# A spectral block's forward and backward pass: full tiles for one-row operands, half-column pairs as fill, and new hand-written orders

## The chip, the cores and the metric

The kernel runs on one core of a Trainium2 chip. A core has a matrix engine (TensorE, "PE" in the rows of the profile, with its weight loads as "PEld"), a vector engine (VectorE, "DVE"), a scalar engine (ScalarE, "ACT"), a general engine (GpSimd, "POOL") and a queue engine that only starts transfers (SyncE, "SP"). The metric is the time on the device in microseconds (us). The median of three runs of the kernel before the change is 398.4 us (397.93 to 398.51). The profiled execution is a single one and has its own time.

## The reference

The kernel computes one block's output and all its gradients, in bf16, with S = 2048 rows, D = 512 columns and F = 1792 hidden columns:

```python
mod = (silu(c) @ w_mod)               # six rows of 512: sa, ca, ga, sb, cb, gb
h   = layernorm(x) * (1 + ca) + sa
x   = x + ga * irfft2(rfft2(h) * (w_r + 1j * w_i))
h   = layernorm(x) * (1 + cb) + sb
out = x + gb * (relu(h @ w1 + b1) ** 2 @ w2 + b2)
```

It returns `out` and, for a given gradient of `out`, the gradients of x, w_r, w_i, w1, b1, w2, b2, c and w_mod. The gradient of w_mod is the outer product of silu(c) with six column sums over all 2048 rows; the gradient of c needs the same sums.

## The kernel before, in words

The 2048 rows are 16 row tiles of 128 (NT), in four row blocks of 512 (NB); the 1792 hidden columns are 14 chunks of 128 (NFC). Both Fourier transforms are matmuls with tables of sines and cosines that the kernel makes itself. PE's work, in time:

- **Start, to about 17 us.** Loads of c, w_mod, x, the output's gradient (`gT`, transposed by the load, four blocks) and w2 (`w2T`, transposed too, four parts). Ten matmuls of constants run first (L731 to L733). `vrow`, the row c, is transposed to a column; silu of it multiplies the blocks of w_mod (`mod_row`, L754, and for block 5 L769, which gives `gb2x`, the factor of the output's gradient). Block 5 is loaded from ACT's queue, the rest from SP's.
- **First spectral product, to about 51 us.** For each pair of row tiles: statistics and scaling of the layernorm, a fold on DVE (L267, L268), the product with the table TA (psA, L303 and L304). As fill, `back_products` (L858): for each row block b and chunk fc, four matmuls 128x128 by 128x512 give w2 transposed times the scaled gradient. `scale_g` (L777) scales `gT` first. At the end of the stage one-row products make `dcrow` (psd, L837) and the columns `mcol` (L842).
- **spec_f23, forward, 51 to 75 us.** Eight groups; each has 16 matmuls psB (L345, 128 rows by 64 columns of the array, in pairs side by side at column 0 and 64), an evaluation AE on ACT (L349), a small patch of AE on POOL (L351), then two times four matmuls psC (L328, also 128 by 64), cast on ACT (Xs, L329) and multiplied with the filter on DVE. Two matmuls of one row (`dcrow` by `ind`, L340) add the shift in the first group. Back products are the fill.
- **spec_g1, 75 to 84 us.** The inverse transform's first part, psG (L375), 64 rows by 128 columns.
- **MLP forward and backward, 84 to 263 us.** Products of 128 by 128 by 512 (L1029, L1059 and others), with column sums (`colsums`, L924) of 32 columns each, four side by side, into one PSUM tile `acc`. After it, rows 0, 32, 64 and 96 of `acc` are the sums for four blocks of w_mod; they are copied to `grow` and `gcrow`.
- **Backward spec_f23 and spec_g1, 263 to 324 us.** The same matmuls as forward; the fill is `grad_w1` (L1303): 16 units of 16 matmuls, eight of 512 columns and eight of 384. `grad_b1` (L1254) goes with one of them. `GMod.emit` (L478) spreads one row of `grow` over 128 partitions with a one-row matmul, then multiplies (ACT, DVE) and writes the gradient of w_mod.
- **Row gradient and grad_w2, 324 us to the end.** Products for the gradient of x, with column sums (L1460), `grad_w2` (L1402) as fill, and the last two `GMod.emit`, from `acc1_sb`.

What runs when is written out by hand. `ORDER` has a list for each engine: the program issues its instructions in some order, and the list names them by their number in it; `set_order` ties each to the one before it on its engine. SP's list is thus the order in which transfers are started. No planner takes part when the kernel is built.

A tile on the array is given by the operand's rows and the weights' columns, and by `tile_position`; rows such as `128*64` in the profile name it.

Of the kernel before, what the change touches and what calls it, by code (L numbers as in the profile page):

```python
# [18 lines left out]
D = 512  # L19
# [3 lines left out]
NFC = 14  # L23
# [50 lines left out]
def build_basic(tc, constp):  # L74
# [14 lines left out]
    K["one0"] = one0  # L89
    pid = constp.tile([P, 1], I32, name="pid")  # L90
# [168 lines left out]


# [199 lines left out]
class GMod:  # L460
# [12 lines left out]
    def emit(self, jc, q, row, pool, ppool, nbuf=2, last=False):  # L473
# [4 lines left out]
        nc.tensor.matmul(psb, lhsT=K["ones_sq"][q:q + 1, :], rhs=row, start=True, stop=True, tile_position=(q, 0))  # L478
# [49 lines left out]
    ),  # L528
    "ACT": (
# [79 lines left out]
def kernel(  # L609
# [703 lines left out]
    for fp in range(0, NFB, 2):  # L1313
        for dc in range(4):
            for fb in (fp, fp + 1):
                units.append(lambda fb=fb, dc=dc: grad_w1(fb, dc))
# [261 lines left out]
```

## Time and profile before

| | |
|---|---|
| median of the runs | 398.4 us |
| profiled execution, its own time | 397.56 us |
| its span in the trace | 395.8 us |
| mean granted clock of TensorE | 0.983 |
| PE, DVE, ACT, POOL busy | 96%, 86%, 69%, 6% |
| instructions in the lists: PE, ACT, DVE, POOL, SP | 2749, 458, 774, 84, 310 |

The shares are means over stages with different limits, so the stages are to be read one by one. A matmul's busy time in a row runs from its start to its modelled end, so that consecutive matmuls overlap in it: the distance from one row's start to the next is what a matmul costs. "x4" in a timeline row means that four instructions in succession are put into one row.

### The profile page before, as it was taken

What the parts mean: (1) busy time and instruction counts of PE and PEld (TensorE: products, weight loads), DVE (VectorE), ACT (ScalarE), POOL (GpSimd) and SP (SyncE); (2) the same over time, 40 slices, a digit from 0 to 9 for tenths busy, and PEclk for the clock granted to TensorE, in tenths of its full rate; (3) what the DMA queues carried; (4) which work ended last, traced back from release to release, by engine and by line L of the source; (5) the groups of instructions that cost most, each with busy time, mean ns of one, the idle gap of its engine ahead of it and who ended that gap; (6) DMA issues with size and microseconds to landing.
All of it is one profiled execution on the core that took longest, in us unless ns stands there. A gap on an engine that the chain in (4) does not pass through costs nothing.

```text
span 395.8 us, 7650 instructions
## 1 busy us (share of the span) xinstructions
PE 379.5 (96%) x2723; PEld 189.0 (48%) x2749; DVE 339.8 (86%) x830; ACT 274.6 (69%) x489; POOL 22.5 (6%) x88
## 2 busy tenths in 40 slices
PE   4799999899999999999999999999999999999996
PEld 1255554455544444444444445446455565444454
DVE  4999978959998689988899899984898998999572
ACT  4469899979973189338824977538837569998482
POOL 7411001000000000000000000000002000000000
PEclk8599999999999999999999999999999999999999
DMA  8997999979389999979966777969999898999998
GB/s 277 215 195 202 276 207 211 335 174 284 99 228 217 226 229 255 187 171 215 246 149 108 217 183 195 300 188 252 333 249 304 238 310 196 180 242 233 285 294 293
DMA packets 141965, 91.00 MB, mean 230 GB/s; under 512 B 96098, under 2 KB 127848, under 8 KB 141416
## 3 DMA queue, kind: packets, MB, share of 16 engines
q1 hardware_dynamic: 141220, 89.93, 91.6%
q10 hardware_dynamic: 708, 0.59, 0.5%
q8 instruction: 21, 0.34, 0.3%
q14 instruction: 16, 0.13, 0.1%
HBM read 36.35 MB, written 33.19 MB: 176 GB/s over the span
## 4 chain that ended last, share of the span: by engine, by line
PE 70%; ACT 10%; DMA 6%; DVE 6%; issue 5%; POOL 1%; ACTq 0%; SPq 0%; POOLq 0%
PE og_0s L1059 11%; PE og_1s L1059 11%; PE mm_0s L1303 5%; PE mm_1s L1402 5%; PE mm_0s L1402 5%; PE mm_0s L858 4%; PE mm_1s L858 4%; PE mm_1s L1029 3%; DMA h_dram<-h2r 3%; PE mm_0s L1029 2%; PE mm_1s L1303 2%; DMA wm_2s<-in_w_mod_dram 2%; PE pst L1029 2%; DMA hn_0s<-h_dram 2%; PE psB L345 2%
## 5 line engine op out<-in xcount | busy, mean ns | idle before, releaser
L1029 PEld LDWEIGHTS <-w 128*128 128x128 bf16 x224 | 21.5, 98 | 26.9 <-issue 2.6
L1303 PEld LDWEIGHTS <-h_sb 128*128 128x128 bf16 x256 | 23.6, 98 | 21.7 <-issue 1.9
L1059 PEld LDWEIGHTS <-gab 128*128 128x128 bf16 x224 | 21.7, 98 | 25.1 <-DVE gab L1036 0.2
L858 PEld LDWEIGHTS <-w2T 128*128 128x128 bf16 x224 | 20.8, 98 | 23.8 <-issue 5.6
L1303 PE MATMUL mm_0s<-gab,h_sb 128*128 128x384 bf16 (+1 forms) x160 | 31.1, 343 | 0.0
L1059 PE MATMUL og_0s<-w1T,gab 128*128 128x512 bf16 x111 | 26.4, 379 | 0.1
L1059 PE MATMUL og_1s<-w1T,gab 128*128 128x512 bf16 x106 | 25.7, 379 | 0.2
L349 ACT ACTIVATE AE<-psB 128x1024 bf16<-128x1024 f32 x16 | 21.7, 1359 | 1.3 <-DMA LFb<-LF_dram 0.9
L1029 PE MATMUL mm_1s<-h2T,w 128*128 128x512 bf16 x84 | 21.7, 379 | 0.6 <-ACT r_1s L1030 0.4
L1303 PE MATMUL mm_1s<-gab,h_sb 128*128 128x512 bf16 (+1 forms) x96 | 22.2, 371 | 0.0
L1029 PE MATMUL mm_0s<-h2T,w 128*128 128x512 bf16 x80 | 21.1, 379 | 0.0
L858 PE MATMUL mm_0s<-gT_0s,w2T 128*128 128x512 bf16 x56 | 16.6, 396 | 1.2 <-DVE gT_0s L777 1.1
L858 PE MATMUL mm_1s<-gT_0s,w2T 128*128 128x512 bf16 x56 | 16.2, 389 | 0.4 <-ACT gab L862 0.3
L1029 PE MATMUL pst<-h2T,w 128*128 128x512 bf16 x60 | 15.9, 379 | 0.0
L858 PE MATMUL mm_0s<-gT_1s,w2T 128*128 128x512 bf16 x56 | 15.0, 379 | 0.0
L858 PE MATMUL mm_1s<-gT_1s,w2T 128*128 128x512 bf16 x56 | 14.9, 379 | 0.1
L1402 PE MATMUL mm_0s<-g_sb,hn_1s 128*128 128x512 bf16 x62 | 14.7, 379 | 0.1
L1072 ACT CAST G_0s<-og_0s 128x512 bf16<-128x512 f32 x4 | 2.3, 587 | 16.2 <-PE og_0s L1059 16.2
L1402 PE MATMUL mm_1s<-g_sb,hn_0s 128*128 128x512 bf16 (+1 forms) x62 | 13.0, 352 | 0.3 <-DMA hn_0s<-h_dram 0.2
L862 ACT CAST gab<-mm_1s 128x512 bf16<-128x512 f32 x20 | 11.9, 594 | 2.0 <-PE mm_1s L858 1.9
L391 PEld LDWEIGHTS <-utcs 128*128 128x128 bf16 x128 | 9.6, 98 | 7.3 <-issue 1.6
L351 POOL TENSOR_TENSOR AE<-AE,one 64x8 bf16<-64x8 bf16 x16 | 6.8, 427 | 93.4 <-ACT AE L349 93.4
(630 smaller groups left out, 1013.5 us busy)
## 6 DMA issues: line engine op xcount, KB each, us to landing
w<-in_B_w_dram SPq DMA_DIRECT2D x2, 1792.0 KB
Z<-wz_dram SPq DMA_DIRECT2D x4, 514.0 KB, 5.3
Xb<-xs_dram SPq DMA_DIRECT2D x4, 514.0 KB, 5.5
x_sb<-in_A_x_dram SPq DMA_DIRECT2D x2, 1024.0 KB
n_dram<-x_sb SPq DMA_DIRECT2D x4, 512.0 KB, 3.8
h_dram<-h2r SPq DMA_DIRECT2D x8, 256.0 KB, 3.6
h_sb<-h_dram SPq DMA_DIRECT2D x4, 512.0 KB, 5.2
g_sb<-in_grad_out_dram SPq DMA_DIRECT2D x2, 1024.0 KB
```

The lines of the kernel that those rows point to most:

```text
L345: nc.tensor.matmul(ps[64 * cs:64 * cs + 64, hh, b, P * e:P * e + P], lhsT=UT[:, c, 2 * (2 * gi + hh) + b, :, :], rhs=K["Cd"][:, P * c:P * ...
L349: nc.scalar.activation(dst, ps.rearrange("p r b (e f) -> p (r b) e f", e=2), AF.Copy, scale=EF_S)
L351: nc.gpsimd.tensor_tensor(end[:, :, 256::-256], end[:, :, 0:1].broadcast_to([64, 4, 2]), K["one0"][64:P, None, :].broadcast_to([64, 4, 2]) ...
L391: nc.tensor.matmul(ps[:, P * i:P * i + P], lhsT=CS[:, i, t].rearrange("p a b -> p (a b)"), rhs=K["Cf"][:, i, :], start=True, stop=True)
L858: nc.tensor.matmul(ps, lhsT=w2T[:, dc, fc * P:(fc + 1) * P], rhs=gT[b][:, :, dc, :], start=(dc == 0), stop=(dc == 3))
L862: nc.scalar.copy(out=gaT[b][:, fc, :], in_=ps)
L1029: nc.tensor.matmul(ps, lhsT=w1[:, dc, (fc + i) * P:(fc + i + 1) * P], rhs=h2T[b][:, :, dc, :], start=(dc == 0), stop=(dc == 3))
L1059: nc.tensor.matmul(ps, lhsT=lhs(fc), rhs=rhs[:, fc, :], start=(fc == 0), stop=(fc == NFC - 1))
L1072: nc.scalar.copy(out=st["G"][:, j % 2, :], in_=P_.pop(j))
L1303: nc.tensor.matmul(blocks(ps, fb), lhsT=h2_sb[:, t, dc * P:(dc + 1) * P], rhs=gh_rows(t, fb), start=(t == 0), stop=(t == NT - 1))
L1402: nc.tensor.matmul(ps[:, 0:w], lhsT=hns[fc][:, t, :], rhs=g_sb[:, t, c:c + w], start=(t == 0), stop=(t == NT - 1))
```

## The change

- **One-row operands as full tiles.** `GMod.emit` multiplies a selector tile `sel` (ones in row 32q of its q-th part, zero elsewhere) with the whole tile instead of one row with a row of ones; `grow`, `acc1_sb`, `brow`, `dcrow`, `ind`, `pm` and `srow` get 128 rows, with zeros set on POOL where nothing is written; psd gets its weights broadcast to 128 columns; the transpose of b1 is 128 by 128. The column sums are copied from `acc` by one DVE instruction, and `gcrow` is gone.
- **Half-column pairs.** `halves` gives two slices of 64 columns. 14 of the 56 units of back products (numbers 23 to 36) and the first 13 of the 16 units of grad_w1 are issued as pairs.
- **Loads.** Block 5 of w_mod is loaded from SP's queue, ahead of blocks 0 and 1.
- **Constants.** 30 matmuls of constants instead of 10.
- **Orders.** All five lists are new: PE 3033 instructions, ACT 456, DVE 772, POOL 95, SP 311. SP's begins with the first half of x, then blocks 5, 0 and 1 of w_mod, the second half of x, the table Cd, `gT` block 0 and three parts of `w2T`; before, it began with the first half of x, blocks 1 and 0, Cd, `gT` block 0, a part of `w2T`, and then the second half of x. PE's gathers matmuls of one tile shape: counted in the lists, 118 runs of one shape before, 55 after. On DVE, four of the row statistics stand ahead of `gb2x`.

The diff's core, without the lists:

```diff
+def halves(split):
+    return [(slice(64 * c, 64 * c + 64), {"tile_position": (0, 64 * c)}) for c in range(2)] if split else [(slice(0, P), {})]
...
-        nc.tensor.matmul(psb, lhsT=K["ones_sq"][q:q + 1, :], rhs=row, start=True, stop=True, tile_position=(q, 0))
+        nc.tensor.matmul(psb, lhsT=K["sel"][:, q // 32, :], rhs=row, start=True, stop=True)
...
-    load_mod(nc.scalar, 5)
+    load_mod(nc.sync, 5)
...
-    for k in range(10):
+    for k in range(30):
...
-    psd = psM.tile([1, D], FP32, name="mod_ps", bufs=1)
+    psd = psM.tile([P, D], FP32, name="mod_ps", bufs=1)
...
-            nc.tensor.matmul(psd[:, P * co:P * co + P], lhsT=sacol[:, k, i:i + 1], rhs=K["Cd"][:, fs], start=(i == 0), stop=(i == 3))
+            nc.tensor.matmul(psd[:, P * co:P * co + P], lhsT=sacol[:, k, i:i + 1].broadcast_to([P, P]), rhs=K["Cd"][:, fs], start=(i == 0), stop=(i == 3))
...
-                nc.tensor.matmul(ps, lhsT=w2T[:, dc, fc * P:(fc + 1) * P], rhs=gT[b][:, :, dc, :], start=(dc == 0), stop=(dc == 3))
+                for m, pos in halves(23 <= NFC * b + fc < 37):
+                    nc.tensor.matmul(ps[m], lhsT=w2T[:, dc, fc * P + m.start:fc * P + m.stop], rhs=gT[b][:, :, dc, :], start=(dc == 0), stop=(dc == 3), **pos)
...
-        nc.vector.tensor_copy(grow[0:96, :], acc[0:96, :])
-        gcrow = h2p.tile([1, D], BF16, name="gcrow")
-        nc.scalar.copy(out=gcrow, in_=acc[96:97, :])
+        nc.vector.tensor_copy(grow, acc)
...
+    sel = lf2.tile([P, 4, P], BF16, name="sel")
+    nc.gpsimd.memset(sel, 0.0)
+    for q in range(4):
+        nc.gpsimd.memset(sel[32 * q:32 * q + 1, q, :], 1.0)
...
-            nc.tensor.matmul(blocks(ps, fb), lhsT=h2_sb[:, t, dc * P:(dc + 1) * P], rhs=gh_rows(t, fb), start=(t == 0), stop=(t == NT - 1))
+            for m, pos in halves(split):
+                nc.tensor.matmul(blocks(ps[m], fb), lhsT=h2_sb[:, t, dc * P + m.start:dc * P + m.stop], rhs=gh_rows(t, fb), start=(t == 0), stop=(t == NT - 1), **pos)
...
-                units.append(lambda fb=fb, dc=dc: grad_w1(fb, dc))
+                units.append(lambda fb=fb, dc=dc, split=len(units) < 13: grad_w1(fb, dc, split))
```

More of the change, by code (lines that the diff above doesn't have):

```diff
@@ L89, in build_basic @@
     K["one0"] = one0
+    pm = constp.tile([P, 2], BF16, name="pm")
+    nc.gpsimd.memset(pm, 0.0)
+    for k in range(2):
+        nc.gpsimd.memset(pm[0:1, k:k + 1], 1.0 - 2 * k)
+    K["pm"] = pm
     pid = constp.tile([P, 1], I32, name="pid")
@@ L497 @@
     "PE": (
[30 rows of a table removed]
[33 rows of a table added]
     ),
     "ACT": (
[13 rows of a table removed]
[14 rows of a table added]
     ),
     "DVE": (
[24 rows of a table removed]
[24 rows of a table added]
     ),
     "POOL": (
[L571 to L572 removed]
+        "14 12 11 21 28 0 25 22 33 4 48 27 1 37 10 34 6 13 47 15 18 20 26 23 7 19 30 24 17 44 46 40 16 8 36 53 78 56 49 54 57 55 "
+        "50 29 41 35 39 38 60 42 2 58 32 31 52 59 5 43 45 61 64-65 51 62 3 63 66-70 9 71-77 80-81 79 83-84 82 86-88 85 89-94"
     ),
     "SP": (
[10 rows of a table removed]
[10 rows of a table added]
     ),
@@ L657 @@
     AEs = make_ae(nc, lfp)
-    dcrow = lfp.tile([1, D], BF16, name="dcrow")
-    ind = lfp.tile([1, NT, 4], BF16, name="ind")
+    dcrow = lfp.tile([P, D], BF16, name="dcrow")
+    ind = lfp.tile([P, NT, 4], BF16, name="ind")
     nc.vector.memset(ind, 0.0)
-    nc.vector.memset(ind[:, :, 0:1], 1.0)
+    nc.vector.memset(ind[0:1, :, 0:1], 1.0)
     gen = Slots(tc, name="gen", bufs=1, side="right")
@@ L689 @@
     x_sb = p0.tile([P, NT, D], BF16, name="x_sb")
-    rows18 = p0.tile([32 + NFC, P], BF16, name="vrow")
-    vrow, brow = rows18[0:4, :], rows18[32:32 + NFC, :]
+    vrow = p0.tile([4, P], BF16, name="vrow")
+    brow = p0.tile([P, P], BF16, name="brow")
+    nc.gpsimd.memset(brow, 0.0)
     nc.scalar.dma_start(vrow, c.rearrange("b (dc p) -> (b dc) p", p=P))
@@ L726 @@
     load_gT(nc.sync, 3)
-    nc.scalar.dma_start(brow, B_b1.rearrange("(fc p) -> fc p", p=P))
+    nc.scalar.dma_start(brow[0:NFC, :], B_b1.rearrange("(fc p) -> fc p", p=P))
     UT = utcs.tile([P, 4, 32, NT, 4], BF16, name="utcs")
@@ L746 @@
     nc.vector.tensor_copy(scf, sc)
-    srow = gall[0:1, 1, :]
+    srow = gall[:, 1, :]
     def mod_row(j):
@@ L761, in mod_row @@
         else:
-            s4, p4 = (a.rearrange("o (k d) -> o k d", k=4) for a in (srow, ps[0:1, :]))
+            s4, p4 = (a.rearrange("o (k d) -> o k d", k=4) for a in (srow, ps))
             nc.scalar.copy(out=s4[:, 0:4:2, :], in_=p4[:, 0:4:2, :])
@@ L820 @@
         mod_row(j)
-    pb = psM.tile([P, NFC], BF16, name="sm_ps", bufs=1)
-    nc.tensor.transpose(pb, brow, K["ident"][32:32 + NFC, 32:32 + NFC])
-    nc.vector.tensor_copy(b1col, pb)
-    pm = constp.tile([1, 2], BF16, name="pm")
-    nc.vector.memset(pm[:, 0:1], 1.0)
-    nc.vector.memset(pm[:, 1:2], -1.0)
+    pb = psM.tile([P, P], BF16, name="sm_ps", bufs=1)
+    nc.tensor.transpose(pb, brow, K["ident"])
+    nc.vector.tensor_copy(b1col, pb[:, 0:NFC])
+    pm = K["pm"]
     psc = psM.tile([P, 8, 2], FP32, name="sm_ps", bufs=1)
@@ L836 @@
             k = int(i in neg)
-            nc.tensor.matmul(psd[:, P * co:P * co + P], lhsT=sacol[:, k, i:i + 1], rhs=K["Cd"][:, fs], start=(i == 0), stop=(i == 3))
+            nc.tensor.matmul(psd[:, P * co:P * co + P], lhsT=sacol[:, k, i:i + 1].broadcast_to([P, P]), rhs=K["Cd"][:, fs], start=(i == 0), stop=(i == 3))
     nc.vector.tensor_scalar(dcrow, psd, 128.0, None, op0=ALU.mult)
     psc = psM.tile([P, 2, 4], FP32, name="sm_ps", bufs=1)
-    for i, row in enumerate((modb[0:1, SB_B, :], modb[0:1, CB1_B, :])):
+    for i, row in enumerate((modb[:, SB_B, :], modb[:, CB1_B, :])):
         for cc in range(4):
@@ L906 @@
     grow = constp.tile([P, D], BF16, name="grow")
+    nc.gpsimd.memset(grow, 0.0)
     nc.sync.dma_start(grow[0:1, :], B_b2[None, :])
     psb2 = mmps.tile([P, D], FP32, name="mm")
-    nc.tensor.matmul(psb2, lhsT=K["ones_sq"][0:1, :], rhs=grow[0:1, :], start=True, stop=True)
+    nc.tensor.matmul(psb2, lhsT=K["ones_sq"], rhs=grow, start=True, stop=True)
     nc.scalar.copy(out=grow, in_=psb2)
@@ L1224 @@
     lf2 = Slots(tc, name="lf2", bufs=1, side="right")
+    sel = lf2.tile([P, 4, P], BF16, name="sel")
+    nc.gpsimd.memset(sel, 0.0)
+    for q in range(4):
+        nc.gpsimd.memset(sel[32 * q:32 * q + 1, q, :], 1.0)
+    K["sel"] = sel
     fin = Slots(tc, name="fin", bufs=2, side="right")
@@ L1298, with grad_w1 @@
     w1o = {}
-    def grad_w1(fb, dc):
+    def grad_w1(fb, dc, split):
         ps = mmps.tile([P, SB], FP32, name="mm")
         for t in range(NT):
-            nc.tensor.matmul(blocks(ps, fb), lhsT=h2_sb[:, t, dc * P:(dc + 1) * P], rhs=gh_rows(t, fb), start=(t == 0), stop=(t == NT - 1))
+            for m, pos in halves(split):
+                nc.tensor.matmul(blocks(ps[m], fb), lhsT=h2_sb[:, t, dc * P + m.start:dc * P + m.stop], rhs=gh_rows(t, fb), start=(t == 0), stop=(t == NT - 1), **pos)
         a, n = FBS[fb]
@@ L1324 @@
     gms = [(j, lambda j=j, q=q, row=row: gm.emit(j, q, row, gmp, mmps))
-           for j, q, row in ((5, 0, grow[0:1, :]), (2, 32, grow[32:33, :]), (3, 64, grow[64:65, :]), (4, 0, gcrow))]
+           for j, q, row in ((5, 0, grow), (2, 32, grow), (3, 64, grow), (4, 96, grow))]
     with Slots(tc, name="f23b", bufs=2) as fr, Slots(tc, name="ewb", bufs=1) as ew:
@@ L1511 @@
         K["Tsb"] = nc.scalar.copy(out=acc1_odd, in_=acc1[64:128, :]).ins
-        acc1_sb = endp["q"].tile([64, D], BF16, name="acc1_sb", bufs=1)
-        nc.vector.tensor_tensor(acc1_sb, acc1[0:64, :], acc1_odd, op=ALU.add)
+        acc1_sb = endp["q"].tile([P, D], BF16, name="acc1_sb", bufs=1)
+        nc.gpsimd.memset(acc1_sb[64:P, :], 0.0)
+        nc.vector.tensor_tensor(acc1_sb[0:64, :], acc1[0:64, :], acc1_odd, op=ALU.add)
         row_end(*pair)
@@ L1516 @@
         for j in range(2):
-            gm.emit(j, 32 * j, acc1_sb[32 * j:32 * j + 1, :], endp["q"], psX, 4, True)
+            gm.emit(j, 32 * j, acc1_sb, endp["q"], psX, 4, True)
             fill(1)
```

2 lines of the change are left out of this document (removed), and 158 rows, old and new, of the table ORDER.

## The prediction

> **What bounds the kernel now.** I read the page's engine shares first, then a table of stretches cut where the kernel changes stage, then the waits of TensorE and VectorE, the chain of waits, and the timeline at the places the change touches.
>
> ```profile
> PE 379.5 (96%) x2723; PEld 189.0 (48%) x2749; DVE 339.8 (86%) x830; ACT 274.6 (69%) x489; POOL 22.5 (6%) x88
> ...
> PEclk8599999999999999999999999999999999999999
> ```
>
> ```profile
> core 0: us, PE busy (x) PEld busy (x) DVE busy (x) ACT busy (x) POOL busy (x), PEclk, DMA share, GB/s
> 7.70:21.40 13.70, 9.05 (x43) 3.80 (x44) 11.13 (x39) 5.48 (x11) 4.63 (x12) 0.50 1.08 238
> 24.90:51.30 26.40, 26.29 (x154) 13.98 (x153) 25.17 (x90) 21.93 (x36) 3.25 (x7) 1.00 0.92 236
> 52.40:74.80 22.40, 21.34 (x234) 10.56 (x232) 19.28 (x47) 22.29 (x33) 3.08 (x8) 1.00 1.01 247
> 74.90:84.40 9.50, 9.16 (x209) 5.83 (x209) 8.94 (x17) 7.12 (x13) 0.00 (x0) 1.00 1.08 202
> 84.40:263.20 178.80, 176.99 (x951) 82.79 (x963) 160.38 (x346) 114.60 (x210) 0.15 (x2) 1.00 0.85 204
> 263.20:323.60 60.40, 60.05 (x671) 32.72 (x667) 49.61 (x113) 39.03 (x63) 3.75 (x8) 1.00 0.97 276
> 323.60:395.80 72.20, 67.81 (x426) 34.90 (x429) 55.96 (x132) 56.16 (x114) 0.00 (x0) 1.00 1.01 249
> ```
>
> TensorE (PE) has no room from 24.9 us on, with one exception: in 52.4 to 74.8 ScalarE (ACT) is busy 22.29 of 22.40 us and PE waits at its end. Before 24.9 us PE waits for loads and VectorE (DVE), and runs at clock 0.50 from 7.7 to 21.4 us. So a gain needs PE time saved in a dense stage, or an earlier start.
>
> A dense PE still loses time where the tile shape (rows*columns used by a matmul, as the rows print it) changes:
>
> ```profile
> 61.27 0.39 PE L858 MATMUL mm_0s<-gT_0s,w2T 128*128 128x512 bf16 x1
> 61.59 0.41 PE L328 MATMUL psC_1s<-AE,LF 128*64 128x257 bf16 x4
> 61.94 0.39 PE L858 MATMUL mm_0s<-gT_0s,w2T 128*128 128x512 bf16 x1
> 62.16 0.81 PE L858 MATMUL mm_1s<-gT_0s,w2T 128*128 128x512 bf16 x3
> 62.91 0.64 PE L345 MATMUL psB<-Cd,utcs 128*64 128x128 bf16 x16
> 63.38 0.39 PE L328 MATMUL psC_0s<-AE,LF 128*64 128x257 bf16 x4
> ```
>
> The first column is the start. Full matmuls of 512 follow each other at 61.94 and 62.16, 0.22 us apart; the one at 61.27 is followed by a half-column one 0.32 us later: the switch cost 0.10. The four matmuls of psC, two side by side, need 2 x 0.107 (257 of 512 columns' 0.216) and took 0.35: 0.13 for the switch back. From psB to psC, both 128*64, nothing shows (16 in 0.47 us). I take **0.10 us a switch**, the lower of the two.
>
> In a sentence that the sum doesn't need: the Trainium skill, "TensorEngine Tiling (Array Packing)", Key Properties, says that a change of tiling mode drains TensorE, and "TensorE: Matmul & The Clock Gate", Single matmul latency, gives a fixed part of 398 cycles at 2.4 GHz, 0.17 us by my estimate if a drain exposes all of it. The rows agree that it costs and show 0.10 to 0.13; by 0.17 the 31 switches that count below would give 5.3 us instead of 3.15.
>
> **The change part by part.** *Tile shapes.* I followed the old and new orders written out for PE and counted runs of one shape: 118 before, 55 after. Three edits do it. One-row operands become full tiles (GMod's, ind/dcrow, grow, mcol, psd, all of other shapes before); 14 units of back products and 13 units of grad_w1 become half-column pairs, so that they join psB and psC; the orders gather what is left. Switches saved by stretch: 7 before 51.3 us, 25 in the forward spec_f23, 5 in spec_g1, 3 in 84 to 263, 17 in the backward spectral stage, 6 after it.
>
> ```profile
> 263.24 0.64 PE L345 MATMUL psB<-Cdb,utcs 128*64 128x128 bf16 x16
> 263.81 3.19 PE L1303 MATMUL mm_0s<-gab,h_sb 128*128 128x512 bf16 x14
> ...
> 267.95 0.38 PE L478 MATMUL mm_1s<-grow,ones_sq 1*128 1x512 bf16 x1
> ...
> 378.29 0.39 PE L478 MATMUL mm<-acc_sb,ones_sq 1*128 1x512 bf16 x1
> 378.61 0.50 PE L1402 MATMUL mm_1s<-g_sb,hn_0s 128*128 128x256 bf16 x3
> ```
>
> These are what is saved: psB into full matmuls, and L478's single rows (0.32 to the next instead of 0.22, so 0.10 here too). 263 to 324: 17 x 0.103 = 1.75; PE is busy 60.05 of 60.40 there, all counts. End: 6 x 0.10 = 0.6. 84 to 263: 0.3. spec_g1: 0.5; DVE is busy 8.94 of 9.50 there, so this could be 0, and up to 1.5 if the 0.8 us wait at its head (below) goes.
>
> *Forward spec_f23: 25 switches, 2.6 us, taken at **nothing**.*
>
> ```profile
> 52.37 1.35 ACT L349 ACTIVATE AE<-psB 128x1024 bf16<-128x1024 f32 x1 [0.39 <-PE psB L345]
> 74.24 0.60 ACT L329 CAST Xs_3s<-psC_1s 128x514 bf16<-128x514 f32 x1
> PE psG_0s L375 <- ACT Xs_3s L329: 0.8, 1, 0.8
> ```
>
> ACT works from the first AE to the last Xs without a gap, and then PE waits for that Xs. In the new ACT order the same instructions stand between these two (8 AE, 16 Xs, 6 gab casts), so PE's saving becomes waiting for ACT. If that is wrong it is worth up to 2.6 us.
>
> *Half-column pairs.* 56 matmuls become 112 and 208 become 416, each of 64 columns, two side by side. No row shows a pair of 512 at 128*64; the nearest are the pairs of 257 above and fours of 512:
>
> ```profile
> 153.37 0.38 PE L924 MATMUL acc<-gp_0s,ones_q 128*32 128x512 bf16 x1
> ...
> 153.80 0.38 PE L924 MATMUL acc<-gp_1s,ones_q 128*32 128x512 bf16 x1
> ...
> 154.12 0.61 PE L1029 MATMUL mm_1s<-h2T,w 128*128 128x512 bf16 x2
> ```
>
> Two fours stand between the first rows: 0.43 / 2 = 0.216 per four, the price of one full matmul. So a pair costs 0.216 (lower end, taken, as both neighbours run side by side) or, one after the other, 0.43. The doubled weight loads hide: psB's 8 pairs with 16 loads took 0.47 us, 59 ns a pair, under 216. (The Trainium skill's tiling page, Restrictions, says that column tiling disables Fast Weight Load; psB's 59 ns with its loads is the answer that this trace gives.)
>
> *POOL's 11 new memsets*, at POOL's mean of 22.5 / 88 = 0.26 us, are 2.8 us on an engine 6% busy: hidden, save 3 ahead of pid, some 0.5 us on a path that PE's constants now cover.
>
> *The start.*
>
> ```profile
> 1.32 8.28 DMA wm_2s<-in_w_mod_dram
> PE sm_ps L769 <- DMA wm_2s<-in_w_mod_dram: 2.8, 1, 2.8
> DVE gb2x L771 <- PE sm_ps L769: 2.5, 1, 2.5
> 10.27 0.16 DVE L771 TENSOR_SCALAR gb2x<-sm_ps 128x4 f32<-128x4 f32 x1 [2.50 <-PE sm_ps L769]
> DMA packets 157, 1.04 MB, mean 205 GB/s; under 512 B 14, under 2 KB 32, under 8 KB 32
> DMA packets 1668, 1.65 MB, mean 358 GB/s; under 512 B 83, under 2 KB 1665, under 8 KB 1665
> 10.00:15.00 5.00, 3.97 (x18) 1.22 (x15) 4.73 (x16) 0.69 (x1) 1.87 (x4) 0.50 1.12 200
> 17.18 2.04 PE L858 MATMUL mm_0s<-gT_0s,w2T 128*128 128x512 bf16 x4 [1.12 <-DVE gT_0s L777]
> 24.88 1.03 PE L858 MATMUL mm_0s<-gT_0s,w2T 128*128 128x512 bf16 x4
> 47.64 0.41 DVE L268 TENSOR_TENSOR fold_u_1s<-h_1s 128x512 bf16<-128x512 bf16 x1
> 49.33 1.05 PE L837 MATMUL mod_ps<-Cd,sacol 128*1 128x128 bf16 x16
> 51.28 0.30 PE L345 MATMUL psB<-Cd,utcs 128*64 128x128 bf16 x4
> ```
>
> The two lines of packets are the stretches from 0 to 5.1 and from 5.1 to 9.7 us. Gate block 5 takes 8.3 us in its queue beside the others, and DVE stands behind gb2x from 7.77 to 10.27, though the first half of x (1.05 MB) was in by about 5.1. After, that load is on SP's queue right behind this half, and ACT's queue keeps only the two small rows. In DVE's order four bn_stats come ahead of gb2x, and it can begin them at about 7.2, as some memsets of before now stand later. From 10.27 to 48.05, the end of the last fold, DVE is full (25.17 of 26.40 in the table), so the chain is 37.8 us; the new order has 1.8 us more in it (memsets and casts that stood elsewhere): 7.2 + 39.6 = 46.8, 1.25 earlier.
>
> On SP three mod blocks (0.52 MB each), all of x and Cd now precede gT_0 and w2T's first part: 4.7 MB to the latter's end. By 9.7 us 2.69 MB had moved; the other 2.0 MB at 238 GB/s (7.7 to 21.4) end at 18.2, and with the scaling the first back product moves from 17.18 to about 20. Until then PE has 30 constants, mod rows and the first psA, which fill what before were waits. Counting its new list by the durations of the old rows at full clock, it reaches at 23.7 the work that it had done at 24.88: 1.2 us earlier. DVE and PE agree; with 4 switches between there and the first AE (psd, ind/dcrow: 0.4) that AE starts at 50.8 instead of 52.37, **1.6 us**. Upper bound 2.5: DVE's 3.1 us less 1.8, and the 1.1 us wait for gT_0 or most of the 7 switches. Lower: 1 us lost if the loads bind.
>
> *At nothing:* the column sums copied once by DVE instead of by DVE and ACT (same 512 columns, and DVE has 10 us of room in the next stage), broadcast weights in psd (16 loads beside 16 matmuls that take 1 us), full rows in srow (as many columns as one row). Without cover each is under 0.7 us.
>
> *Sum.* 1.6 + 0 + 0.5 + 0.3 + 1.75 + 0.6 = 4.75. The profiled execution took 397.56 us (span 395.8, 1.76 around it): 392.8. It lies 0.84 under the median of the runs, so **393.6 us**.
>
> **The rivals.**
> *All switches count (0.17).* If ACT's stretch is stretched by PE, 2.6 more: 391.0. For: 0.39 us of wait before the first AE; against: 22.29 of 22.40.
> *The start gains nothing (0.20).* gT_0 and w2T come late enough to eat it, and the clock, fallen at 7.7 before, falls again: 393.6 + 1.6 = 395.2, or up to 396.2. For: gT_0 behind 2 MB more at the 238 GB/s of 7.7 to 21.4. Against: PE has other work till 20 us. (The skill's clock page, Part 1, has a free-running window of about 3.4 us, full clock after a busy one; the constants would bring it at 8 to 12 us instead of 21.4. This trace shows only the late one.)
> *DMA holds the last two stages (0.09).* DMA share 0.97 and 1.01 there; if what PE saves is waited for at the loads, 2.35 is lost: 395.9.
> *Slower: the queue on SP (0.10).* Each us of lateness of w2T's first part past about 20 us takes PE's fill away; when the first AE comes after 56.3 (52.37 plus 3.15 from the other stages plus 0.8), all is lost. That needs the first back product at about 25.5: the queue's 4.7 MB from 1.3 us on at the 200 GB/s of 10 to 15 us end at 24.8, and scaling comes behind; PE, short of work till then, starts cold and needs 7 us more at half clock. **399.6**. For: loads that transpose set that 200. Against: only the last 0.9 MB of the 4.7 transpose, and 358 GB/s were reached before.
> *It doesn't do what it says: the pairs run one after the other (0.02).* 56 x 0.216 + 112 x 0.216 + 96 x 0.162 = 52 us, less what ACT's bound hides: about 440.
>
> **How the numbers follow.** The forecast has 0.42. No change is within 0.2%, 0.8 us, about what can be told: 397.6 to 399.2. Faster: 0.42 + 0.17 + 0.18 + 0.05 = 0.82, with the tails of the start and DMA cases in "same" 0.07; slower 0.11. The range reaches from all switches with the start's best (391.0 - 0.9 and another 0.6 from spec_g1, 389.5) to just under no change, 398.3. The forecast's own range is 392.2 to 395.
>
> **What would show it.** After: rows of L858 and L1303 as 128*64 pairs 0.216 apart; psB into them without the 0.10; the stretch from the first AE to the last Xs still 22.4 us and ACT full; the backward stage 58.6 us instead of 60.4; the first AE near 50.8, gb2x no longer waiting, gT_0 landing near 18; clock 1.0 well before 21. It is wrong if the first AE comes after 52.4, if spec_f23 shrinks by 1 us or more, or if a pair takes over 0.25.

## The result

The changed kernel is not faster: its median is 402.6 us (400.5 to 405.0, four runs) against 398.2 us, a ratio of 1.0112 (95% interval 1.0065 to 1.0158). Measured once more on another chip, in eleven runs, it took 400.4 us (397.2 to 403.6) against 398.1, a ratio of 1.0025 (0.9977 to 1.0073). The ratios leave out runs over 1.5% above the fastest of their kernel, the medians and ranges don't, so a ratio isn't exactly the quotient of two medians. So the changed kernel lies between no measurable change and 1.1% slower. Its spread goes with the clock: of the eleven runs, the four with a mean granted clock of 1.000 took 397.2 to 398.9 us, the seven with 0.991 or 0.996 took 399.2 to 403.6. The profiled execution took 404.99 us, of which the span is 403.1.

The page of the changed kernel has nearly the same engine shares as before, and one new dip of the clock, near five sixths of the span:

```profile
PE 382.6 (95%) x3033; PEld 200.9 (50%) x3033; DVE 341.2 (85%) x828; ACT 273.2 (68%) x488; POOL 26.7 (7%) x99
...
PEclk9999999999999999999999999999999979999999
```

These are stretches cut near the same events as before, with one exception: the second row ends where the last Xs starts, while before the change it ended where that Xs ended, 0.6 us later. The columns are start and end, length, then busy time and instructions of PE, PEld, DVE, ACT and POOL, the clock, the DMA share and GB/s:

```profile
24.90:51.60 26.70, 26.70 (x164) 14.64 (x161) 25.90 (x93) 21.99 (x37) 5.42 (x10) 1.00 0.86 226
52.40:74.00 21.60, 20.19 (x288) 13.45 (x284) 19.60 (x50) 21.55 (x32) 3.68 (x9) 1.00 0.85 183
74.00:84.00 10.00, 9.01 (x212) 5.82 (x211) 9.15 (x17) 7.55 (x15) 0.00 (x0) 1.00 0.81 258
84.00:263.00 179.00, 178.58 (x986) 83.53 (x981) 162.04 (x350) 114.37 (x210) 1.28 (x6) 1.00 0.84 208
263.00:321.20 58.20, 57.60 (x866) 38.61 (x862) 48.17 (x111) 37.84 (x61) 3.41 (x9) 1.00 0.99 261
321.20:403.10 81.90, 70.79 (x439) 36.31 (x433) 58.02 (x133) 57.32 (x115) 0.52 (x1) 0.95 0.96 239
```

The backward spectral stage, 60.2 us before, is 58.2: that gain is there. The row-gradient stage, 72.3 us before, is 81.9: nearly all of the loss is in this one stage, and PE is busy in it hardly longer than before (70.8 us against 67.8, most of the difference at half clock). What PE waits for there, in its list of waits from 320 us on, and the rows of the engines behind them:

```profile
PE psT_1s L401 <- ACT Tsb_1s L403: 3.9, 1, 3.9
PE acc L1479 <- DVE q_1s L1497: 2.0, 1, 2.0
PE mm_1s L1421 <- ACT gw_0s L1422: 0.8, 1, 0.8
PE mm_0s L1421 <- DMA hn_1s<-h_dram: 0.3, 1, 0.3
```

```profile
327.97 0.60 ACT L403 ACTIVATE Tsb_1s<-psT_1s 128x512 bf16<-128x512 f32 x1 [4.52 <-DMA out_dram<-Xb]
...
377.99 0.69 DVE L1497 TENSOR_TENSOR q_0s<-gh_0s,n_0s 128x1024 bf16<-128x1024 bf16 x1 [2.86 <-DMA n_0s<-n_dram]
```

```profile
315.00:327.00 12.00, 9.60 (x151) 5.72 (x146) 7.85 (x17) 4.19 (x8) 0.00 (x0) 1.00 0.97 316
327.20:333.90 6.70, 5.28 (x22) 2.73 (x22) 3.71 (x5) 3.35 (x6) 0.00 (x0) 0.50 0.93 197
```

In these rows psT is the row gradient's transform on PE and Tsb its copy by ACT; n, gxl and g_sb are loaded rows; q is a product whose column sums PE makes; hn is a block of hidden values, loaded transposed for grad_w2, and gw a result of it; Xb holds the filter's gradient and gwm a block of the gradient of w_mod.

All four waits end at transfers. Tsb waits for a store of a filter-gradient tile whose memory it takes; the column sum waits for q_1s, which stands on DVE behind q_0s and the load of n_0s; gw_0s stands on ACT behind gs_3s, which comes behind the same load on DVE's list. After the first wait PE runs at clock 0.50 for 6.7 us.

A sum that explains the length of this stage in the profiles of this study: I add up how much later than its columns allow each matmul starts (gaps over 0.25 us), and half of the time at clock 0.50, from the last psG on. What is left of the stage is 70.0 to 71.5 us, but for the last two kernels below with stores from POOL (68.7 and 68.5).

| kernel | first AE | backward stage | last psG | stage to the end | PE waits in it | at half clock | left |
|---|---|---|---|---|---|---|---|
| before | 52.37 | 60.2 | 323.5 | 72.3 | 1.5 | 0 | 70.8 |
| changed, first profile | 52.44 | 58.1 | 321.2 | 81.9 | 7.8 | 7.7 | 70.3 |
| changed, second chip | 51.84 | 58.2 | 320.6 | 75.9 | 4.4 | 0 | 71.5 |

PE's waits in this stage, by its list of waits (which leaves out short ones and so adds up to less than the table), before the change and then in the second profile of the changed kernel:

```profile
PE mm_1s L1402 <- ACT gw_4s L1403: 0.7, 1, 0.7
PE mm_1s L1402 <- DMA hn_0s<-h_dram: 0.2, 1, 0.2
```

```profile
PE psT_1s L401 <- ACT Tsb_1s L403: 1.6, 1, 1.6
PE acc L1479 <- DVE q_1s L1497: 0.9, 1, 0.9
PE mm_1s L1421 <- ACT gw_0s L1422: 0.8, 1, 0.8
PE mm_0s L1421 <- DMA hn_1s<-h_dram: 0.2, 1, 0.2
```

In the second profile the changed kernel ends at 396.5 us, where the kernel before ended at 395.8: it comes 2.9 us earlier to the last stage and waits 2.9 us longer in it. In the first it waits longer still, and the clock falls.

### The profile page after: what moved, and what is told of

Same layout as the page of the kernel before. It is cut to its first block, busy times and chain, and to the rows that moved or that the text cites. A ratio compares the mean times of both kernels' runs of the same rounds, so it can differ in the third digit from the quotient of the medians.

```text
span 403.1 us, 8231 instructions
## 1 busy us (share of the span) xinstructions
PE 382.6 (95%) x3033; PEld 200.9 (50%) x3033; DVE 341.2 (85%) x828; ACT 273.2 (68%) x488; POOL 26.7 (7%) x99
## 4 chain that ended last, share of the span: by engine, by line
PE 60%; DVE 15%; DMA 9%; ACT 8%; SPq 4%; issue 2%; POOL 1%; ACTq 0%; DVEq 0%; POOLq 0%
PE og_1s L1074 8%; PE og_0s L1074 8%; PE mm_1s L1421 6%; PE mm_0s L1421 5%; PE mm_1s L872 5%; PE mm_0s L872 4%; PE mm_1s L1044 4%; PE mm_0s L1044 3%; ACT AE L359 3%; DMA out_dram<-Xb 2%; PE pst L1044 2%; DMA Xb<-xs_dram 2%; DMA out_dram<-gwm_0s 2%; PE mm_1s L748 1%; PE mm_0s L748 1%
## 5 line engine op out<-in xcount | busy, mean ns | idle before, releaser
L1322 PEld LDWEIGHTS <-h_sb 128*64 128x64 bf16 (+1 forms) x464 | 29.3, 110 | 17.5 <-issue 2.9
L872 PEld LDWEIGHTS <-w2T 128*128 128x128 bf16 (+1 forms) x280 | 22.8, 102 | 20.4 <-issue 2.5
L1322 PE MATMUL mm_0s<-gab,h_sb 128*64 128x384 bf16 (+2 forms) x288 | 32.9, 347 | 0.0
L1074 PE MATMUL og_1s<-w1T,gab 128*128 128x512 bf16 x112 | 27.0, 379 | 0.0
L1322 PE MATMUL mm_1s<-gab,h_sb 128*64 128x512 bf16 (+2 forms) x176 | 22.8, 378 | 0.0
L872 PE MATMUL mm_0s<-gT_0s,w2T 128*64 128x512 bf16 (+1 forms) x76 | 15.2, 380 | 0.5 <-DVE gab L874 0.4
L872 PE MATMUL mm_1s<-gT_0s,w2T 128*128 128x512 bf16 (+1 forms) x72 | 15.3, 381 | 0.0
L872 PE MATMUL mm_0s<-gT_1s,w2T 128*128 128x512 bf16 (+1 forms) x64 | 15.1, 379 | 0.0
L872 PE MATMUL mm_1s<-gT_1s,w2T 128*128 128x512 bf16 (+1 forms) x68 | 14.7, 379 | 0.0
L874 DVE CAST gab<-mm_0s 128x512 bf16<-128x512 f32 x12 | 8.2, 687 | 5.4 <-PE mm_0s L872 5.2
```

Of the source, the lines that this page charges most:

```text
L872: nc.tensor.matmul(ps[m], lhsT=w2T[:, dc, fc * P + m.start:fc * P + m.stop], rhs=gT[b][:, :, dc, :], start=(dc == 0), stop=(dc == 3), **pos)
L874: nc.vector.tensor_copy(out=gaT[b][:, fc, :], in_=ps)
L1074: nc.tensor.matmul(ps, lhsT=lhs(fc), rhs=rhs[:, fc, :], start=(fc == 0), stop=(fc == NFC - 1))
L1322: nc.tensor.matmul(blocks(ps[m], fb), lhsT=h2_sb[:, t, dc * P + m.start:dc * P + m.stop], rhs=gh_rows(t, fb), start=(t == 0), stop=(t == N ...
```

## The experiments

### Single transfers

The first question was whether a few entries of SP's new list do it. In that list seven stores of the first Xb tile stand behind a transposed load of hn_1s, which holds SP for 5 us:

```profile
308.37 5.06 SPq L1235 DMA_TRANSPOSE hn_1s<-h_dram  x1
...
320.76 1.53 SPq L1373 DMA_DIRECT2D out_dram<-Xb  x2
```

**Stores first.**

```diff
 SP's list, by what is started
+out_dram<-Xb (first tile) x7
 n_0s<-n_dram
 out_dram<-Xb (first row)
 hn_1s<-h_dram, transposed
 ...
-out_dram<-Xb (first tile) x7
```

> The changed kernel with one thing different: on SP's list the seven stores of the first filter-gradient tile (Xb, the ones that the changed list starts after the transposed load of hn_1s) stand ahead of that load. Theory (the place of these stores delays ACT's first Tsb, which gets their memory): ACT's 4.5 us wait on out_dram<-Xb and PE's 4.1 us gap at the head of the row-gradient stage go, the clock no longer falls to 0.5 for two windows there (3.4 us), and the time is 395 to 397.5 us. Rival (the transfers as a whole bind, as the backward stage now ends 2.1 us sooner): the gap comes back at another load within some 10 us and the time stays above 400 us.

Measured: 401.0 us (398.4 to 406.1), ratio 1.0056 (1.0019 to 1.0093). PE's wait for Tsb is gone, and another has come:

```profile
PE mm_1s L1421 <- DVE g_sb L1443: 2.5, 1, 2.5
PE acc L1479 <- DVE q_1s L1497: 2.3, 1, 2.3
```

That is the rival's sign: 6 us later in the stage PE waits for g_sb. Its waits add up to 6.4 us. The theory fell.

**Stores and loads first.** As that, and two n loads and the load of hn_1s ahead of a w_mod load and a store near 369 us.

> As the kernel with the stores moved, and on SP's list the last two n loads and the load of hn_1s stand ahead of the w_mod load and the gw store that the changed list starts first. Theory (SP's order): DVE's 2.9 us wait for n_0s and PE's gaps of 2.2 and 1.5 us near 380 us go as well: 393 to 394.5 us, or 2 to 3 us less than the kernel with the stores alone. Rival (transfers as a whole): within 0.7 us of that kernel.

Measured: 402.3 us (401.7 to 403.4), ratio 1.0112 (1.0052 to 1.0173). The wait for q_1s went; one of 1.3 us for a gw tile and one of 0.7 us for hn_2s came; 5.9 us in all. The theory fell here too.

**The hn_1s load late.** This time the load itself moves:

```diff
 SP's list, by what is started
-hn_1s<-h_dram, transposed
 out_dram<-gwm, LGb, gxl, n, g_sb, out_dram<-Xb ... (16 entries)
+hn_1s<-h_dram, transposed
```

> The changed kernel; on SP's list one entry moves: the transposed load of hn_1s, which stands in SP for 5 us at 308 us, goes behind the 16 entries that follow it (the last two gwm stores, the Xb stores, the n, gxl and g_sb loads). Theory D (this load, started 9 us earlier than before, makes all behind it late: gwm stores, then g_sb, whose memory they hold; Xb stores, then Tsb): both PE gaps at 320 to 335 us go (4.1 or 2.7 us), no cold window there, stage after the last psG 73 to 76 us, time 396 to 398.5. Rival B (too much to transfer in this time, whatever the order): the gap comes back between 320 and 345, time within 1 us of the changed kernel's 400.5 to 402.5.

Measured: 403.5 us (400.1 to 405.1), ratio 1.0112 (1.0074 to 1.0150). Tsb's wait fell to 1.7 us, and the next hn tile was late instead:

```profile
PE mm_1s L1421 <- DMA hn_0s<-h_dram: 3.2, 1, 3.2
PE psT_1s L401 <- ACT Tsb_1s L403: 1.7, 1, 1.7
```

**The same, and the late loads earlier.**

> As the kernel with the hn_1s load late, and the last two n loads and the loads of hn_1s and hn_2s that the changed list has at 370 to 383 us stand ahead of the w_mod load and stores near 369 us. Theory A (order alone): PE's waits for q_1s and for hn near 380 us (3.7 us) go too, 394 to 396 us, faster than before. Rival B: within 0.7 us of the kernel with only hn_1s moved, the waits moving to other loads.

Measured: 404.4 us (399.5 to 408.5), ratio 1.0098 (1.0046 to 1.0150). There is no gain: its profile, of a run of 408.2 us, has waits of 5.0 us for a gw tile and of 2.6 for hn_0s.

**The kernel before, with this load early.** The one entry goes from behind the first g_sb load to ahead of the gwm store.

> The kernel before; on SP's list one entry moves: the transposed load of hn_1s goes from 317.4 us to ahead of the gwm store at 308.9 us, about where the changed list has it. Theory D: the g_sb load, 315.4 us before, is started some 4 us later, PE waits 2 to 5 us between 325 and 340, time 400 to 403 us. Rival: the place of this one load doesn't matter, within 0.7 us of before.

Measured: 398.8 us (397.2 to 400.3), ratio 0.9990 (0.9955 to 1.0025). The place of this load is not the cause; that theory fell in both directions. Each time one transfer was put right, another was late.

### The lists exchanged

**Changed kernel, SP's old order from 262 us on** (132 entries; the text below counts 131).

> The changed kernel; the last 131 entries of SP's list (every transfer from 262 us on) stand in the order that they have in the kernel before, all else is as changed. Theory A (the new order of SP's list makes the loads of the row-gradient stage late): the stage from the last psG to the end, 72.3 us before and 78 to 82 in the changed kernel, is 72 to 74 us, PE's waits in it fall from 6 to 8 us to 2 or 3, and the time is 395 to 397 us. Theory B (the transfers bind as a whole, since the backward stage is 2 us shorter): stage of 74.5 to 76 us, time 397.5 to 399, the 2 us of the stage before given back. Theory C (the new orders of DVE, ACT and PE make the stage long): unchanged, 78 us or more, above 400 us.

**Kernel before, SP's new order from 262 us on.**

> The kernel before, with the order of SP's list from 262 us on taken from the changed kernel and nothing else. Theory A: the stage from the last psG to the end grows by 4 to 8 us from 72.3, time 402 to 406 us. Theories B and C: within 1 us of before.

Measured: 416.9 us (415.6 to 419.4), ratio 1.0489 (1.0464 to 1.0514), and 408.2 us (406.8 to 408.5), ratio 1.0266 (1.0248 to 1.0285). Theory A had foreseen the second and the opposite of the first: both mixtures are slower than both kernels. SP's list is fitted to the lists of the other engines, the new one to the new ones, and the experiment can't say which of the lists is at fault. It does say how much the order of the transfers alone can cost here: 11 us in the kernel before, 14 or more in the changed one.

### Less to transfer

**Without eight stores** (blocks of the gradient of w_mod, 2.1 MB).

> The changed kernel without the eight stores of the gradient of w_mod that are made before the row-gradient stage (blocks 5, 2, 3 and 4, 256 KB each, 2.1 MB in all, some 8 us at 250 GB/s); these blocks of the output are not written. Theory B (transfers as a whole): the stage falls by most of the 4 to 6 us that it lost, time below 397.5 us. Theory A (order): the stall at the first Tsb stays or shrinks by no more than the eight starts on SP's queue (0.45 us each, of which those ahead of the Xb stores count): 399 us or more.

Measured: 397.3 us (395.8 to 399.3), ratio 0.9997 (0.9980 to 1.0015). The time is theory B's, by a hair. The profile, of a run of 398.6 us, doesn't decide: PE still waits 5.2 us in it, but the clock falls no more before 395 us.

**Both kernels without 38 stores** (these eight and the 30 of the filter's gradients, 4.2 MB).

```diff
-            for i, o in enumerate((out_2, out_3)):
+            for i, o in enumerate(()):
...
-            nc.sync.dma_start(self.out9_view[:, dc:dc + 2, cs], gwm)
+            if last:
+                nc.sync.dma_start(self.out9_view[:, dc:dc + 2, cs], gwm)
```

> The kernel before without 38 stores of the stages from 263 us on: the eight gwm stores (gradient of w_mod, blocks 5, 2, 3, 4) and the 30 stores of the filter's gradients from Xb, 4.2 MB and 38 starts on SP's queue in all; these outputs are not written. Theory B (the transfers set when the row-gradient stage can go on; before, PE's work and the transfers end together): PE waits 1.5 us in that stage, so no more than that is gained: 396.5 to 398.5 us. Rival C (the changed kernel's lists for PE, ACT and DVE are what makes the stage long): the same here.

> The changed kernel without the same 38 stores. Theory B: PE's waits after the last psG, 4.4 to 7.8 us, fall to 1 to 2.5 and no cold window is left there; the stage is 71.5 to 73.5 us and what the backward stage gained is kept: 392.5 to 395 us, 3 to 4.5 less than the kernel before without these stores. Rival C: waits of 4 us or more stay, time not below the kernel before without these stores.

Measured: the kernel before 397.3 us (396.5 to 398.4), ratio 0.9994 (0.9975 to 1.0014), no gain; the changed one 393.7 us (393.4 to 394.0), ratio 0.9910 (0.9886 to 0.9934). The two stages of the changed kernel, and then those of the kernel before, each with the columns of the stage table:

```profile
263.30:321.50 58.20, 57.24 (x861) 38.24 (x860) 47.92 (x111) 37.68 (x61) 3.74 (x9) 1.00 0.93 237
321.50:392.10 70.60, 67.01 (x436) 35.23 (x435) 57.70 (x133) 57.22 (x115) 0.53 (x1) 1.00 0.94 237
```

```profile
264.40:324.60 60.20, 59.85 (x668) 32.61 (x666) 49.33 (x112) 38.87 (x62) 3.58 (x8) 1.00 0.79 227
324.60:396.60 72.00, 67.76 (x433) 35.12 (x435) 56.14 (x132) 56.11 (x115) 0.00 (x0) 1.00 0.92 232
```

With 4.2 MB less to move, PE waits 0.3 us in the changed kernel's last stage, and what it gained is kept: 3.6 us between the medians, 4.5 between the spans. The kernel before gains nothing: its waits in this stage go from 1.5 us to 1.1. So what the changed kernel loses hangs on its transfers, and not on the new lists of PE, ACT and DVE alone (rival C).

The stores left out are those that Tsb and g_sb wait for, so the same was done with others.

**Without 23 other stores** (grad_w1 and most of grad_w2, 3.6 MB); those of Xb and gwm stay.

> The changed kernel without 23 other stores: the eight of grad_w1 and 15 of grad_w2 (some 3.6 MB, 23 starts), which hold no memory that Tsb or g_sb needs; the stores of Xb and of gwm stay, at their places. These outputs are not written. Sum of the transfers (theory B): PE's waits after the last psG fall to 2.5 us or less, 394 to 396.5 us, as with the 38 other stores left out. The two memory dependencies (Tsb behind the Xb stores, g_sb behind the gwm stores): 2 us or more of waits stay between 320 and 335 us, time 397.5 or more.

Measured: 394.8 us (392.6 to 397.4), ratio 0.9928 (0.9895 to 0.9961).

```profile
PE psT_1s L401 <- ACT Tsb_1s L403: 1.8, 1, 1.8
```

This is the only wait left from 300 us on. So part of both holds: the time is that of theory B, as the waits near 380 us went with the load on the queues, and Tsb's wait for the Xb stores, about 2 us, stayed with these stores at their places.

**Twelve stores from POOL's queue**, nothing left out: the second Xb tile's, 5.4 us of starts on SP.

```diff
-                        K["gW"] = nc.sync.dma_start(v[:, b, :, a:a + n, :].rearrange("u h g f -> u h (g f)"),
+                        K["gW"] = (nc.gpsimd if gi == 7 else nc.sync).dma_start(v[:, b, :, a:a + n, :].rearrange("u h g f -> u h (g f)"),
...
-                            K["gW"] = nc.sync.dma_start(v[:, 1 - b, 1 - h, 16 - a:16 - a - n:-1, :], X[64 * b + 32:64 * b + 64, h]).ins
+                            K["gW"] = (nc.gpsimd if gi == 7 else nc.sync).dma_start(v[:, 1 - b, 1 - h, 16 - a:16 - a - n:-1, :], X[64 * b + 32:64 * b + 64, h]).ins
```

> The changed kernel; the 12 stores of the second Xb tile are started from POOL's queue instead of SP's, nothing is left out. Theory B1 (SP's queue, where a start takes 0.45 us and a transposed load 2 to 6, is what is late): its 5.4 us in SP are free, PE's waits after the last psG fall by 2 us or more, time 396 to 398. Theory B2 (the transfers themselves, DMA share 0.9 to 1.1): waits unchanged within 1 us or moved, 400 to 403.

Measured: 400.0 us (399.2 to 402.1), ratio 1.0072 (1.0041 to 1.0102). The waits near 380 us shrank to 0.4 us, but Tsb's was 2.7, and the clock fell behind it; neither theory has this in full. Two more kernels added the moves of above to it:

> The changed kernel with the 12 stores of the second Xb tile started from POOL and the seven stores of the first one ahead of hn_1s's load on SP's list: nothing is left out. If the order of starts can take what the sum of the transfers asks for: PE's waits after the last psG below 3 us, 395 to 397.5 us, faster than before. If the sum of the transfers sets the end (theory B): waits of 4 us or more in other places, 399 to 402.

> As that kernel, and the last two n loads and the loads of hn_1s and hn_2s ahead of the w_mod load near 369 us. If the order can do it: 2 us less than the kernel without this; theory B: within 1 us of it.

Measured: 403.3 us, ratio 1.0094 (1.0063 to 1.0125), with PE waiting 4.3 us for g_sb; and 408.2 us, ratio 1.0216 (1.0163 to 1.0270), with 5.8 us for g_sb and 4.2 for a gw tile. The second is 5 us slower than the first, which neither theory had foreseen. No order of starts that I tried lets the changed kernel keep its gain. Whether it is the bytes or the starts that are too many isn't settled: every kernel that became faster had fewer of both. Nor is a third thing separated: SP's list stops where it waits for memory (from 300 us on in the first profile 3.0 us for an Xb store and 3.4 for a psT matmul; before, 4.2 us at most for one matmul), and fewer stores relieve that too.

**The changed kernel once more.**

> The changed kernel once more, on the chip of these runs. Theory (its time is set by how long PE waits for transfers after 320 us and by whether the clock falls there): 400 to 403 us; stretch from the last psG to the end 76 to 82 us and as much above 72.3 as its PE waits and half of its cold windows add up to, less the 1.5 us of waits before; first AE between 51.2 and 52.5 us, the later the later the clock warms. Rival (a fixed cost somewhere else in the new lists): the sum leaves over 1 us open.

Measured: 400.4 us, as given with the result; the stage to the end took 75.9 us in its profile, and the first AE came at 51.84. Its sum is in the table above: nothing is left open beyond 0.7 us.

### Pairs and the start

**No half-column pairs**, all else as changed:

```diff
-                for m, pos in halves(23 <= NFC * b + fc < 37):
+                for m, pos in halves(False):
...
-            for m, pos in halves(split):
+            for m, pos in halves(False):
```

> The changed kernel and its orders, but all back products and all of grad_w1 are full matmuls (no half-column pairs); runs of one shape go from 3 to 27 in the forward spec_f23 and from 21 to 40 in the backward spectral stage. Theory (0.10 us a switch; the forward stage is bound by ACT): backward spectral stage 1.9 us longer (first psB to last psG 58.1 to 60.0), first AE to last Xs unchanged within 0.4 us (21.55). Rival a (switches count forward too): that stretch 2.4 us longer. Rival b (a pair costs more than a full matmul, or the gain of the backward stage is from the order alone): backward stage not longer by more than 0.5 us. The time as a whole is left to the stall in the row-gradient stage: 399 to 405 us.

Measured: 401.3 us (398.3 to 403.2), ratio 1.0072 (1.0040 to 1.0104).

```profile
51.30:73.90 22.60, 21.61 (x236) 11.06 (x235) 20.14 (x51) 21.75 (x32) 2.96 (x9) 1.00 0.81 183
262.60:322.60 60.00, 59.12 (x658) 32.02 (x660) 47.95 (x111) 37.98 (x61) 3.08 (x9) 1.00 1.01 271
322.60:396.50 73.90, 67.78 (x434) 35.37 (x435) 57.85 (x133) 57.36 (x115) 0.52 (x1) 0.99 0.99 251
```

The backward stage is 60.0 us, 1.9 more than the 58.1 and 58.2 in the two profiles with pairs, for 19 more switches: 0.10 us each, as forecast. (In other profiles with pairs, where a few transfers were moved or left out, this stage takes 57.7 to 59.3 us, so the size is less certain than one pair of profiles makes it look.) The forward stretch from the first AE to the last Xs is 22.6 us instead of 21.55, 1.0 more for 24 switches: neither nothing nor 2.4. The number of switches doesn't explain it alone: the kernel before changes shape there about as often (25 runs of one shape in its trace, 26 here) and needs 21.9. And in this profile, of a run of 398.3 us, the end is at 396.5 us, as in the second profile of the changed kernel, though PE came to the last stage 2.0 us later: waits of 2.9 us instead of 4.4.

**mod_row(1) seven places earlier.**

> The changed kernel, but on PE's list the four matmuls of mod_row(1) stand 7 places earlier, ahead of seven of the constant matmuls. Theory (the constants delay modb, and DVE's chain with it): modb some 2 us earlier, DVE's 1.3 us wait for it gone, first AE at 51.2 us instead of 52.44, all 1.2 us less than the changed kernel in runs of the same kind. Rival (loads or ACT set the start): first AE within 0.3 us of 52.44 and no gain.

Measured: 400.7 us (398.6 to 402.5), ratio 1.0069 (1.0039 to 1.0100). The first AE came at 52.18 us; modb no longer holds DVE, but gb2x does, for 1.7 us instead of 0.7. With full speed from about the same time (11.4 and 11.5 us), the changed kernel without the move has it at 51.84. The same move together with SP's old order:

> As the kernel with SP's old order from 262 us on, and mod_row(1) moved ahead of seven constants on PE's list. Theory on the start (constants delay modb): first AE at 51.2 us or earlier and 0.3 to 1.2 us less than the kernel with SP's order alone. Rival: no difference beyond 0.3 us.

Measured: 418.7 us, ratio 1.0535 (1.0516 to 1.0554), first AE at 52.83. The theory that modb's place behind seven constants holds up the start fell.

## Why the prediction was wrong

Forecast were 393.6 us, faster; measured were 402.6 and, the second time, 400.4.

**The step that failed** is the one from PE's time to the kernel's: "263 to 324: ... PE is busy 60.05 of 60.40 there, all counts" and, for the end, "6 x 0.10 = 0.6". The savings in PE's work are real. The backward stage fell by 2.1 us (forecast 1.75), and in the two kernels without 38 stores what is left of the last stage is 70.0 us instead of 70.9 (forecast 0.6 less; such remainders differ by as much between profiles of one kernel). What failed is that they count: PE came 2.3 us earlier to the last stage in the first profile and 2.9 in the second, and waited 6.3 and 2.9 us longer in it, for transfers. The prediction's own rows have the DMA share at 0.97 and 1.01 in these two stages; before the change PE's work and the transfers ended nearly together, with 1.5 us of waits in 72. With 4.2 MB of stores left out the saved time was kept. The sum also has no term for SP's new order past the start, although the change includes it: put into the kernel before, that order alone cost 11 us. How much of the loss it makes in the changed kernel isn't shown.

**The rival "DMA holds the last two stages"** was the right mechanism, with a chance of 0.09 and the wrong size. It ended at the gain of these stages lost, 395.9 us. The loss went on past that point, in two ways: the transfers came later than before for PE's needs (in the first profile 7.8 us of waits where giving back the 2.3 us would make 3.8; in the second 4.4, which is just the giving back), and behind a long wait the clock fell, so that the first profile loses 3.4 us more at half speed. No step of the prediction has the clock falling at the end of the kernel.

**The start** (forecast 1.6 us) gave between nothing and 1.6, and 1.0 in the middle: the first AE comes at 50.8 to 52.45 us in the fourteen profiles of the changed kernel that leave the start as it is (median 51.65), and at 52.4 to 53.1 in four of the kernel before (52.7). In the first profile, at 52.44, it meets the prediction's own sign of being wrong. DVE begins its statistics at 7.34 us, as forecast (7.2), but the chain of 39.6 us was counted without waits. In the first profile it has 2.6 us of them:

```profile
DVE h_0s L817 <- ACT modb L771: 1.3, 1, 1.3
DVE gb2x L786 <- PE sm_ps L784: 0.7, 1, 0.7
DVE gab L874 <- PE mm_0s L872: 0.6, 1, 0.6
```

The working took PE's list "at full clock". It is at half clock well into the constants, and for how long differs from run to run. Two constants in succession in the first profile, 0.38 us apart and 0.42 to the next, and in that of the kernel without eight stores, 0.22 apart:

```profile
9.92 0.58 PE L748 MATMUL mm_1s<-ones_sq 128*128 128x512 bf16 x1
10.30 0.63 PE L748 MATMUL mm_0s<-ones_sq 128*128 128x512 bf16 x1
10.72 2.53 PE L748 MATMUL mm_1s<-ones_sq 128*128 128x512 bf16 x4
```

```profile
9.89 0.38 PE L749 MATMUL mm_1s<-ones_sq 128*128 128x512 bf16 x1
10.11 0.38 PE L749 MATMUL mm_0s<-ones_sq 128*128 128x512 bf16 x1
10.33 1.67 PE L749 MATMUL mm_1s<-ones_sq 128*128 128x512 bf16 x4
```

The trace's records have full speed from 13.1 us in the one and from 9.7 in the other, and the first AE at 52.44 and 51.18. (The page's row PEclk shows 9 there all the same: ahead of the first record it takes the clock as full.) The other twelve profiles fit between or beside these in the same order, from 8.7 us with the first AE at 50.81, the forecast, to 13.1 with 52.45: each us of later full speed makes the first AE about 0.4 us later. So the forecast start was reached once, where full speed came earliest. The Trainium skill, "TensorE: Matmul & The Clock Gate", Part 1, has the activity window free-running, with about 3.4 us of busy time to full speed. The constants run from 5.41 us on, so it took 3.3 to 7.7 us here: the lower end agrees, the upper is over two such windows. In the kernel before, whose constants run from 1.05 us on, the trace has full speed from 4.3 to 7.7 us, which the prediction's "only the late one" passes over. The rival on SP's queue didn't come: the first back product starts at 20.3 to 21.9 us (forecast about 20), not at 25.5; how that rival's 399.6 follows from its terms the prediction doesn't say.

**The forward spec_f23** was rightly taken as bound by ACT: 25 switches less gave 0.3 us, and ACT is busy 21.55 of 21.60 us. The experiment without pairs refines it: there the stretch is 1.0 longer and ACT is busy 21.75 of 22.60, so that ACT has to wait.

**The pairs** run side by side, as forecast. In this timeline eight half-column matmuls take 0.86 us, 0.215 a pair, and psB joins them without a gap that shows:

```profile
63.84 1.03 PE L872 MATMUL mm_1s<-gT_0s,w2T 128*64 128x512 bf16 x8
64.70 0.62 PE L355 MATMUL psB<-Cd,utcs 128*64 128x128 bf16 x16
65.14 1.03 PE L872 MATMUL mm_0s<-gT_0s,w2T 128*64 128x512 bf16 x8
```

spec_g1 (forecast 0.5) and the MLP (0.3) gave nothing: from the last Xs to the last psG it takes 10.0 us before and after, and from there to the backward stage 179.0 and 179.1.

**The sum as a whole** was 4.75 us. Between the spans of the two kernels without 38 stores it is 4.5, between their medians 3.6. That it comes so near is in part luck: of the 4.5 us, the start makes 0.9 (forecast 1.6), the forward spec_f23 0.4 (nothing), spec_g1 and the MLP together nothing (0.8), the backward stage 2.0 (1.75) and the end 1.4 (0.6), of which 0.8 are waits. The sum held, by terms that miss in both directions, for a kernel that this one is not.

## What to carry to other kernels

When a row of the profile shows the bound engine full and the transfers' share near 1 in the same stage, the saved time of a faster engine may not be the gain: ask first what would have to land sooner, and give "the gain is waited for" a larger chance than 0.09. The share alone doesn't decide it, as the forward spec_f23 stands at 1.01 too and is set by ACT. A cheap test is to leave out a few stores: if the changed kernel becomes faster and the old one doesn't, transfers take the gain. And an order of starts that is fitted to one set of lists can't simply be carried over to another: here the exchange cost 11 us and more.

## What the hardware showed

A wait of PE can cost more than itself. In the twenty profiles here, from 25 us on, all twelve waits of 2.6 us or more came with a fall of the clock to 0.50, in the wait or within 1.3 us after it, for one or two stretches of 3.4 us. Of the twelve waits from 2.0 to under 2.6 us seven came with one, within 1.6 us, and five did not: the same wait can cost 1.7 us more in one execution and nothing in another. Single waits of 1.6 to 1.8 us came with none. Two waits of 1.0 and 0.8 us close together had 3.4 us at half clock behind them in one profile (below), while 0.9 and 0.8, in the second profile of the changed kernel, had none. The Trainium skill, "TensorE: Matmul & The Clock Gate", Part 1, names an idle window of about 3.4 us before the clock falls; by these waits less idle time than that can be enough.

```profile
380.42 0.38 PE L1479 MATMUL acc<-q_1s,ones_q 128*32 128x512 bf16 x1 [1.02 <-DVE q_1s L1497]
...
381.60 3.17 PE L1421 MATMUL mm_1s<-g_sb,hn_0s 128*128 128x256 bf16 x15 [0.79 <-ACT gw_0s L1422]
```

These two rows are of the kernel with the hn_1s load late: the 15 matmuls of 256 columns are busy for 3.17 us, against 1.80 in the first profile of the changed kernel, where they run at full speed.
